# Regrouping exponent, score, attended-value and projection matmuls in a windowed attention kernel: bursts of three and three with six exponent buffers

## The chip, the cores and the metric

The kernel runs on one core of one Trainium2 chip, as one launch. The metric is the device time in microseconds. The core has five engines with queues of their own: TensorE (PE, with its weight loads shown as PEld), VectorE (DVE), ScalarE (ACT), GpSimd (POOL) and SyncE (SP), which here only issues DMAs. Each engine works through its own instructions in the order in which the program holds them, and waits on semaphores for the others.

## The reference

The input has 2048 tokens of 576 features. Four layers are added to it in turn: attention, spectral filter, attention, spectral filter.

```python
def _A_ref(x, wqkv, wo):
    B, S, D = x.shape
    H = 32; Dh = D // H; W = 256
    qkv = (x @ wqkv).reshape(B, S, 3, H, Dh).transpose(2, 0, 3, 1, 4)
    q, k, v = qkv[0], qkv[1], qkv[2]
    scores = jnp.einsum("bhqd,bhkd->bhqk", q, k) * (Dh ** -0.5)
    idx = jnp.arange(S)
    mask = (idx[:, None] - idx[None, :] >= 0) & (idx[:, None] - idx[None, :] < W)
    p = _softmax(jnp.where(mask[None, None], scores, -1e9), axis=-1)
    o = jnp.einsum("bhqk,bhkd->bhqd", p, v)
    return o.transpose(0, 2, 1, 3).reshape(B, S, D) @ wo

def _B_ref(x, w_r, w_i):
    X = jnp.fft.rfft2(x, axes=(-2, -1)) * (w_r + 1j * w_i)
    return jnp.fft.irfft2(X, s=x.shape[1:], axes=(-2, -1))

x = x + _A_ref(_layernorm(x), A_wqkv, A_wo)
x = x + _B_ref(_layernorm(x), B_w_r, B_w_i)
x = x + _A_ref(_layernorm(x), A_wqkv, A_wo)
x = x + _B_ref(_layernorm(x), B_w_r, B_w_i)
```

A query thus sees the 256 keys up to its own position, that is three tiles of 128 keys for each tile of 128 queries.

## The kernel before, in words

The program is written out by hand: every engine's order is the order of the calls in the Python code. `layer_a` is the attention, `layer_b` the spectral filter, and each is called twice. The change lies in `layer_a`, in its second part (from line 762 on), which the profile shows as the stretch of L801, L857, L889 and L909.

The 32 heads are taken in eight groups of four (`n`, `NQ` = 8), and a group in 16 tiles of 128 tokens (`i` or `j`, `NT` = 16). A step of the main loop (line 955) has a number t from -10 to 129, and x = t stands for the pair (group, tile) in order, 128 of them. A head has 18 features; a matrix of queries or keys stands in 64 rows, in which the high and the low part of the numbers lie one below the other. Two heads (`hp` = 0 and 1) stand in the upper and the lower 64 rows of the same tile, and `pair` tells two such couples apart. So four heads are two couples, and the matmuls of hp 0 and hp 1 use different halves of TensorE's rows.

These are the pieces of work of a step:

- `score_max(x, pair, hp)` (line 846): a matmul (L857, tile S, three PSUM buffers) gives the scores of 128 queries against up to 384 keys, and VectorE (L859) adds the mask and takes the row's maximum into `m`. It runs ten steps ahead (`LEAD` = 10).
- `m_rows(n, c)` (line 862): after four tiles a transpose (L865, tpm) turns the maxima into rows, ScalarE negates them (L867, mt) and four DMAs on SP (L872) put them into row 63 of each head's queries, so that the next matmul subtracts the maximum by itself. Line 864 takes the transpose's PSUM buffer from those of S.
- `exps(x, pair, hp)` (line 877): a matmul (L889, tile E, three PSUM buffers) gives the scores once more, keys in the rows and up to 384 queries in the columns, less the maximum; ScalarE (L890) takes the exponent into one of four places of tile P. After the fourth, two selections on POOL (L892 and L895) set what the mask excludes to zero. P has five buffers.
- `pv(x)` (line 900): sixteen short matmuls (L909) collect the attended values of four heads in U, one PSUM bank, in two halves: the keys of the tile before with 256 queries, and those of the tile itself or of the one before the last with 128. After four tiles ScalarE copies U out (L914, us). It runs two steps behind `exps`.
- `norm(n, c)` (line 916): four transposes (L919, tpo, in a buffer of S), a reciprocal (L922) and a product (L924) on VectorE, and a store on SP (L929).
- The steps of the projection (`pj`, line 943): 392 matmuls of 512 columns (L801), 14 to a block of queries or keys, into one PSUM bank. The 14th is followed by a cast on ScalarE (L813), and by `remainders()` (line 783), in which VectorE subtracts the cast (L816) and SP stores both parts (L818). The first 14 blocks' tile `sg` takes one of P's buffers. `goal` (lines 946 to 950) says how many projection matmuls are done by each step; 84 lie before t=2, and the other 308 are spread over t=2 to about t=102.
- `stack_load(n, c)` (line 824): twelve DMAs on SP (L833) that bring queries and keys of a group's quarter into place, twenty steps ahead. `v_load` brings the values. In the first layer 16 DMAs on POOL (line 992) copy constants to another place, one every four steps from t=32.

A step is written out by hand as: two exponents and two scores (hp 0 and 1 each), `pv(t-2)`, two exponents and two scores, about three projection steps, and then at most one of the `m_rows` and `norm` that are due:

```python
for pair in range(2):
    for hp in range(2):
        if 0 <= t < NX: exps(t, pair, hp)
    for hp in range(2):
        if t + LEAD < NX: score_max(t + LEAD, pair, hp)
    remainders()
    if pair == 0 and 0 <= t - 2 < NX: pv(t - 2)
for f in more: f()
```

A step whose t-2 begins a group (a multiple of 16) has no attended values, since the first tile's are taken with the second's.

Of the kernel before, what the change touches and what calls it, by code (L numbers as in the profile page):

```python
# [18 lines left out]
NT = 16  # L19
# [383 lines left out]
NQ = 8  # L403
# [205 lines left out]
def layer_a(tc, ident, eps, bp, src, dst, wqk_d, wv_d, wo_d, dc_d, gc_d, dram, copy, wvs, second, spectral, share):  # L609
# [17 lines left out]
    if True:  # L627
# [134 lines left out]
        with ExitStack() as c2:  # L762
# [24 lines left out]
            def proj(i, c, bank=0):  # L787

                box = {}
                ks = k_steps()  # L790
                cs = slice(c * 512, c * 512 + 512)

                def mm(s, k):
                    wk, p, xk = k
                    if s == 7 and c == 2 and 0 < i < 8:
                        w_split(i + 1)
                    if s == 0:
                        box["ps"] = pp.tile([128, 512], F32, tag="E" if bank else "pj", name=f"pj{i}_{c}", bufs=3 if bank else 1)
                    w = wt[i][0] if p == "h" else wt[i][1]
                    x = tokens(xT(xk, slice(0, S)), c) if second else xT(xk, cs)  # L800
                    T.matmul(box["ps"].rearrange("r (n p) -> r n p", n=NT) if second else box["ps"], w[:, wk], x, start=s == 0, stop=s == len(ks) - 1)  # L801
                    if s == len(ks) - 1:
                        if 4 * i + c < 14:

                            sg = wp.tile([128, 4, 384], F32, tag="P", name=f"sg{i}_{c}", bufs=5)
                            sg = sg.rearrange("r a b -> r (a b)")[:, 0:1024].rearrange("r (a t) -> r a t", a=2).bitcast(F32R)
                        else:
                            sg = wp.tile([128, 2, 512], F32R, tag="sg", name=f"sg{i}_{c}", bufs=2)
                        by, rest = box["ps"], sg
                        if second:  # L810
                            by = by.rearrange("r (n p) -> r p n", n=NT)
                            rest = sg.rearrange("r a (p n) -> r a p n", n=NT)
                        A.copy(rest[:, 0], by)  # L813

                        def remainder():
                            V.tensor_sub(rest[:, 1], by, rest[:, 0].bitcast(F32))  # L816
# [29 lines left out]
            def score_max(x, pair, hp):  # L846
# [30 lines left out]
            def exps(x, pair, hp):  # L877
# [19 lines left out]

            us = {}

            def pv(x):  # L900
                n, i = divmod(x, NT)

                e = i - i % 2
                for j in (i - 1, i - 2 + 2 * (i % 2)):
                    q0 = e if j < i else i
                    q1 = e + 2 if i - 1 == j else q0 + 1
                    for h in range(4):
                        if j >= 0:
                            T.matmul(U[32 * h:32 * h + 19, (q0 % 4) * 128:(q0 % 4) * 128 + 128 * (q1 - q0)], vts[n][:, j, h],  # L909
                                     pt[n, j][:, h, (q0 - j) * 128:(q1 - j) * 128],  # L910
                                     start=j == max(e - 1, 0), stop=j == i or (i == e and j == i - 2), skip_group_check=True)
                if i % 4 == 3:
                    us[n, i // 4] = u = wp.tile([128, 512], F32, tag="us", name=f"us{n}_{i}", bufs=1)
                    A.copy(u, U)  # L914

            def norm(n, c):
                tp = pp.tile([128, 4, 128], F32, tag="S", name=f"tpo{n}_{c}", bufs=3)
# [34 lines left out]
            OB = NX - 8  # L952
            out = Out(nc, ident, eps, bp, ov, o7v, srcv, dstv, wo_d, dc_d, gc_d)
# [1 line left out]
            for t in range(-LEAD, NX + 2):  # L955

                if t + LEAD in (0, 2):
                    stack_load(0, 2 + (t + LEAD) // 2)
                n, c = divmod(t + 20, NT)
                if c % 4 == 0 and 0 < n < NQ:  # L960
                    stack_load(n, c // 4)
                if t + LEAD == 5:
                    v_load(0)
                if t + 12 in range(NT, NX, NT):
                    v_load((t + 12) // NT)

                want = goal.get(t, len(pj))
                ends = done // 14 != want // 14
# [17 lines left out]
                    f()  # L986
                if t >= 1:
                    remainders()
                if copy and t >= 32 and t % 4 == 0 and t < 32 + 16 * len(copy):

                    z, r = divmod(t // 4 - 8, 4)
                    P.dma_start(*[a[32 * r:32 * r + 32] for a in copy[z]])

                y = t + LEAD - 1
                if 0 <= y < NX and y % 4 == 3:
# [102 lines left out]
```

## Time and profile before

| what | value |
|---|---|
| device time, median of three runs | 1575.02 us (1569.77 to 1582.44) |
| span of the profiled execution, first to last instruction | 1561.3 us |
| mean granted clock of TensorE | 0.993 |
| loop t=2 to t=103, first attention layer | 143.0 to 449.2 us |
| the same, second attention layer | 920.1 to 1226.6 us |

The profile is of one execution, whose span is 1561.3 us; its device time isn't listed by itself, and the median of the runs lies 13.7 us above that span. The rows of the profile name the line, the engine, the operation and the tiles as out<-in, then how many there were, their busy time and the mean of one; in the timeline a row begins with the start and the duration in microseconds, and rows of one kind that follow one another are merged. An entry in square brackets is idle time of that engine before the instruction, and what ended it. TensorE's matmuls overlap, and their ends are modelled, so distances between starts say more than durations. The stretches' rows give busy time of PE, PEld, DVE, ACT and POOL with the number of instructions in brackets.

### The profile page before, as it was taken

The numbers are of one execution on the slowest core, as the hardware profiler recorded it, in microseconds if no ns is written. First come the engines' busy times: TensorE is split into PE (matmuls) and PEld (weight loads), VectorE is DVE, ScalarE is ACT, GpSimd is POOL, SyncE is SP. The second block draws the span as 40 slices with busy tenths as digits, with TensorE's granted clock in tenths as the row PEclk, the third lists the DMA queues.
The fourth block names the chain that finished last, engine by engine and source line by source line (L and its number), as shares of the span: only waits on it lengthen the run. The fifth ranks groups of instructions, "written<-read, shape, count | busy, mean of one in ns | idle before, by whom it ended". The sixth has DMA issues, their size and how long they took to land.

```text
span 1561.3 us, 34502 instructions
## 1 busy us (share of the span) xinstructions
PE 1495.4 (96%) x12124; PEld 1086.4 (70%) x12124; DVE 976.1 (63%) x3152; ACT 806.4 (52%) x1900; POOL 624.6 (40%) x1026
## 2 busy tenths in 40 slices
PE   7999999999999899999999999999999998999998
PEld 7975555555555899858999755555555558998598
DVE  4327777777775555455852377777777755554577
ACT  5523666666667344323454246666666673442243
POOL 2172444444446233162321823443443563322434
PEclk9999999999999999999999999999999999999999
DMA  6656455555553456666764564555535543657664
GB/s 196 186 178 213 138 163 175 155 157 171 153 162 99 144 181 193 214 240 226 257 166 96 184 209 136 151 149 148 144 122 144 150 142 116 199 183 248 213 217 137
DMA packets 203130, 267.62 MB, mean 171 GB/s; under 512 B 103183, under 2 KB 108303, under 8 KB 201999
## 3 DMA queue, kind: packets, MB, share of 16 engines
q1 hardware_dynamic: 194638, 245.44, 51.8%
q10 hardware_dynamic: 7680, 15.59, 2.8%
q0 software_dynamic: 640, 4.39, 1.0%
q8 instruction: 97, 1.59, 0.4%
q14 instruction: 75, 0.61, 0.1%
HBM read 166.71 MB, written 102.00 MB: 172 GB/s over the span
## 4 chain that ended last, share of the span: by engine, by line
PE 70%; DVE 7%; DMA 6%; ACT 5%; POOL 5%; issue 1%; SPq 1%; POOLq 0%; DVEq 0%; ACTq 0%
PE pj L801 16%; PE U L909 11%; PE E L889 11%; PE S L857 7%; PE ops L555 6%; PE vps L738 4%; PE pf L202 3%; PE pz L215 3%; DMA ofree<-yd 2%; PE pi L361 2%; PE tpo L919 2%; ACT P L890 2%; PE po L382 2%; DVE ofree L298 1%; POOL uv L302 1%
## 5 line engine op out<-in xcount | busy, mean ns | idle before, releaser
L859 DVE CUSTOM_DVE_ANT_0 jk<-S,mask 128x384 bf16<-128x384 f32 (+2 forms) x1024 | 499.0, 529 | 148.8 <-PE S L857 146.0
L890 ACT ACTIVATE P<-E 128x384 f32<-128x384 f32 (+2 forms) x1024 | 423.2, 474 | 200.6 <-PE E L889 185.3
L892 POOL TENSOR_SCALAR_AFFINE_SELECT P<-P 128x512 f32<-128x512 f32 x256 | 163.0, 637 | 440.1 <-ACT P L890 438.0
L889 PE MATMUL E<-qs,ks 64*128 64x384 f32 (+2 forms) x1024 | 235.6, 429 | 12.4 <-ACT P L890 9.0
L857 PE MATMUL S<-ks,qs 63*128 63x384 f32 (+2 forms) x1024 | 212.3, 351 | 3.2 <-DVE m L859 2.4
L909 PE MATMUL U<-P,vq 128*19 128x128 f32 (+1 forms) x3840 | 204.9, 332 | 1.0 <-POOL P L895 1.0
L889 PEld LDWEIGHTS E<-qs,ks 64*128 64x128 f32 x1024 | 103.7, 184 | 145.3 <-ACT P L890 81.7
L909 PEld LDWEIGHTS U<-P,vq 128*19 128x19 f32 x3840 | 90.5, 98 | 101.3 <-issue 36.3
L801 PE MATMUL pj<-xh,wqh 128*128 128x512 f32 x360 | 158.0, 439 | 2.1 <-ACT vt L742 1.7
L895 POOL TENSOR_SCALAR_AFFINE_SELECT P<-P 128x512 f32<-128x512 f32 x224 | 142.6, 636 | 0.0
L857 PEld LDWEIGHTS S<-ks,qs 63*128 63x128 f32 x1024 | 116.5, 188 | 37.2 <-DVE m L859 27.1
L555 PE MATMUL ops<-oroom 128*128 128x288 f32 x840 | 120.8, 299 | 4.4 <-DVE oroom L538 3.0
L801 PE MATMUL pj<-xh,wql 128*128 128x512 f32 x360 | 122.9, 414 | 0.1
L801 PE MATMUL pj<-xl,wqh 128*128 128x512 f32 x288 | 120.9, 420 | 0.0
L555 PEld LDWEIGHTS ops<-oroom 128*128 128x128 f32 x840 | 112.8, 189 | 6.2 <-DVE oroom L538 4.0
L801 PEld LDWEIGHTS pj<-xh,wqh 128*128 128x128 f32 x360 | 68.0, 189 | 37.3 <-issue 24.2
L816 DVE TENSOR_TENSOR sg<-pj,sg 128x512 fp32r<-128x512 f32 x72 | 49.8, 691 | 61.8 <-ACT sg L813 61.8
L171 POOL TENSOR_TENSOR eo<-xn 128x287 f32<-128x287 f32 x32 | 26.1, 817 | 153.1 <-ACT xn L169 142.1
L859 DVE DVE_READ_ACCUMULATOR2_ANT m<- 128x1 f32 x1024 | 85.2, 83 | 0.0
L813 ACT CAST sg<-pj 128x512 fp32r<-128x512 f32 x72 | 42.4, 588 | 75.4 <-PE pj L801 73.8
L361 PE MATMUL pi<-oroom 128*128 128x256 f32 (+1 forms) x576 | 76.0, 285 | 5.4 <-ACT oroom L346 4.0
L801 PEld LDWEIGHTS pj<-xh,wql 128*128 128x128 f32 x360 | 64.7, 188 | 23.5 <-issue 13.5
(177 smaller groups left out, 2593.7 us busy)
## 6 DMA issues: line engine op xcount, KB each, us to landing
qk_d<-sg SPq DMA_DIRECT2D x56, 512.0 KB
qs<-qk_d SPq DMA_DIRECT2D x384, 72.0 KB
ks<-qk_d SPq DMA_DIRECT2D x384, 72.0 KB
v_d<-vt SPq DMA_DIRECT2D x32, 304.0 KB
vq<-v_d SPq DMA_DIRECT2D x16, 608.0 KB
yd<-ye SPq DMA_DIRECT2D x32, 290.0 KB
wt<-in_w SPq DMA_DIRECT2D x16, 580.0 KB
x<-ofree SPq DMA_DIRECT2D x32, 288.0 KB
```

Of the source, the lines that this page charges most:

```text
L361: T.matmul(o, z[:, sl, c, lo:lo + m], mo, start=k == 0, stop=k == 5)
L555: self.nc.tensor.matmul(self.ps[u][n][:, 0:288], x, self.w[p][:, wk * D + n * 288:wk * D + n * 288 + 288], start=first and i == 0, stop=la ...
L738: T.matmul(ps[:, n, 0:288], xT(xk, c), w[:, wk, n * 288:(n + 1) * 288], start=i == 0, stop=i == len(ks) - 1)
L801: T.matmul(box["ps"].rearrange("r (n p) -> r n p", n=NT) if second else box["ps"], w[:, wk], x, start=s == 0, stop=s == len(ks) - 1)
L816: V.tensor_sub(rest[:, 1], by, rest[:, 0].bitcast(F32))
L857: T.matmul(ps[:, 0:N], q[b:b + 63, pair, i * 128:i * 128 + 128], k[b:b + 63, pair, lo:hi], start=True, stop=True)
L859: V.tensor_tensor_reduce(out=jk[:, 0:N], in0=ps[:, 0:N], in1=mask[:, 384 - N:384], scale=1.0, scalar=-3e38, op0=ALU.add, op1=ALU.max, accu ...
L889: T.matmul(ps[:, 0:nq], k[b:b + 64, pair, j * 128:j * 128 + 128], q[b:b + 64, pair, j * 128:j * 128 + nq], start=True, stop=True)
L890: A.activation(p[:, hl_, 0:nq], ps[:, 0:nq], AF.Exp, scale=SC)
L892: P.affine_select(out=p[:, :, 0:128], in_=p[:, :, 0:128], pattern=[[0, 4], [1, 128]], compare_op=ALU.is_ge, fill=0.0, base=0, channel_mult ...
L895: P.affine_select(out=p[:, :, 256:384], in_=p[:, :, 256:384], pattern=[[0, 4], [-1, 128]], compare_op=ALU.is_gt, fill=0.0, base=0, channel ...
L909: T.matmul(U[32 * h:32 * h + 19, (q0 % 4) * 128:(q0 % 4) * 128 + 128 * (q1 - q0)], vts[n][:, j, h], pt[n, j][:, h, (q0 - j) * 128:(q1 - j) ...
```

## The change

The steps t=2 to t=103 (`MIX` = 104) leave the main loop and are written out by a new function, `bursts()`. The 408 exponents of these steps are taken in order, three at a time, and with each three go three scores, of the tile ten steps on and with the other half of the rows: a score, three exponents, two scores. So there are 136 bursts of six matmuls, in which the halves of the rows alternate. Between bursts stand the attended values and the projection steps in turn: after even bursts halves of `pv` (now `part(x, half)`), mostly three, and after odd bursts five, five or four projection steps, 14 in six bursts. At the starts of head groups an overflow rule puts some halves in front of projection steps. What is due of `norm` and `m_rows` follows the projection steps, up to two at a time, or all but the last where a block of 14 ends. The subtraction of the cast follows the scores of the next burst instead of standing before them. `loads(x)` and `copies(x)` stand ahead of the burst with tile x's first exponent. P has six buffers instead of five, and the room for it in SBUF comes from `dynamic_dma_scratch_size=8192`, a smaller room for the descriptors of POOL's DMAs than the one it has by default. The steps before t=2 and from t=104 on stay as they are, except that there too P has six buffers.

```diff
-                            sg = wp.tile([128, 4, 384], F32, tag="P", name=f"sg{i}_{c}", bufs=5)
+                            sg = wp.tile([128, 4, 384], F32, tag="P", name=f"sg{i}_{c}", bufs=6)
...
-                if t == hp == pair == 0:
+                if (n, c) not in ms:
...
-                    pt[n, j] = wp.tile([128, 4, 384], F32, tag="P", name=f"P{n}_{j}", bufs=5)
+                    pt[n, j] = wp.tile([128, 4, 384], F32, tag="P", name=f"P{n}_{j}", bufs=6)
...
-            def pv(x):
+            def part(x, half):
                 n, i = divmod(x, NT)
                 e = i - i % 2
-                for j in (i - 1, i - 2 + 2 * (i % 2)):
-                    q0 = e if j < i else i
...
+                j = (i - 1, i - 2 + 2 * (i % 2))[half]
+                q0 = e if j < i else i
...
-                if i % 4 == 3:
+                if half and i % 4 == 3:
                     us[n, i // 4] = u = wp.tile([128, 512], F32, tag="us", name=f"us{n}_{i}", bufs=1)
                     A.copy(u, U)
+
+            def pv(x):
+                part(x, 0)
+                part(x, 1)
...
-            for m in range(22):
-                a, b = [2 + 23 * z // 5 for z in (m, m + 1)]
-                for t in range(a, b):
-                    goal[t] = 84 + 14 * m - (-14 * (t + 1 - a) // (b - a))
+            MIX = 104
...
+            def bursts():
+                es = [(x, pair, hp) for x in range(2, MIX) for pair in range(2) for hp in range(2)]
+                ss = [(x + LEAD, pair, 1 - hp) for x, pair, hp in es]
+                left = [*(5, 5, 4) * 20, *(4, 4, 3, 3) * 2]
+                gaps = {}
+                for p in range(2 * MIX - 5):
+                    g = 2 * ((p + 1) // 3)
+                    if p % 8 == 0 and p and (p + 1) % 3:
+                        g += (p + 1) % 3
+                    elif p % 8 == 1 and p > 1 and (p + 1) % 3 == 2:
+                        g += 1
+                    gaps.setdefault(g, []).append(divmod(p, 2))
+                at = done
+                for k in range(len(es) // 3):
+                    e, c = es[3 * k:3 * k + 3], ss[3 * k:3 * k + 3]
+                    for x, pair, hp in e:
+                        if pair == hp == 0:
+                            loads(x)
+                            copies(x)
+                    score_max(*c[0])
+                    for f in e:
+                        exps(*f)
+                    score_max(*c[2])
+                    score_max(*c[1])
+                    remainders()
+                    for x, half in gaps.get(k, ()):
+                        part(x, half)
+                        if half and x % 4 == 3:
+                            due.append((norm, *divmod(x // 4, 4)))
+                    full = (3 * k + 3) // 4 + 11
+                    if (3 * k) // 4 + 11 < full and full % 4 == 3:
+                        due.append((m_rows, *divmod(full // 4, 4)))
+                    if k % 2:
+                        m = left.pop(0)
+                        for f in pj[at:at + m]:
+                            f()
+                        ends, at = at // 14 != (at + m) // 14, at + m
+                        for f, *a in due[:len(due) - 1 if ends else 2]:
+                            f(*a)
+                            due.pop(0)
+                remainders()
+                part(MIX - 3, 1)
+                return at
...
             for t in range(-LEAD, NX + 2):
...
+                if 2 <= t < MIX:
+                    if t == 2:
+                        due.append((m_rows, 0, 2))
+                        done = bursts()
+                    continue
+                loads(t)
...
-    nc = bacc.Bacc("TRN2", target_bir_lowering=False, num_devices=1)
+    nc = bacc.Bacc("TRN2", target_bir_lowering=False, num_devices=1, dynamic_dma_scratch_size=8192)
```

More of the change, by code (lines that the diff above doesn't have):

```diff
@@ L946, in layer_a, with loads @@
             goal = {t: -(-70 * (t + LEAD + 1) // 9) if t < -1 else (75, 80, 84)[t + 1] for t in range(-LEAD, 2)}
-            for m in range(22):
-                a, b = [2 + 23 * z // 5 for z in (m, m + 1)]
-                for t in range(a, b):
-                    goal[t] = 84 + 14 * m - (-14 * (t + 1 - a) // (b - a))
[L952 to L958, printed above, removed]
+            MIX = 104
+            def loads(t):
                 n, c = divmod(t + 20, NT)
@@ L965, in layer_a, with copies @@
                     v_load((t + 12) // NT)
+            def copies(t):
+                if copy and t >= 32 and t % 4 == 0 and t < 32 + 16 * len(copy):
+                    z, r = divmod(t // 4 - 8, 4)
+                    P.dma_start(*[a[32 * r:32 * r + 32] for a in copy[z]])
+            def bursts():
[41 more added lines that the diff above has]
+                return at
@@ L967, in layer_a @@
+            OB = NX - 8
+            out = Out(nc, ident, eps, bp, ov, o7v, srcv, dstv, wo_d, dc_d, gc_d)
+            for t in range(-LEAD, NX + 2):
+                if t + LEAD in (0, 2):
+                    stack_load(0, 2 + (t + LEAD) // 2)
+                if 2 <= t < MIX:
[4 more added lines that the diff above has]
+                loads(t)
                 want = goal.get(t, len(pj))
```

15 lines of the change are left out of this document (6 added, 9 removed).

## The prediction

> **What bounds the kernel now.** I read the page's head first, then the busy times of the stretches of the run, then TensorE's own timeline inside one step of the loop that the change rewrites.
>
> ```profile
> span 1561.3 us, 34502 instructions
> PE 1495.4 (96%) x12124; PEld 1086.4 (70%) x12124; DVE 976.1 (63%) x3152; ACT 806.4 (52%) x1900; POOL 624.6 (40%) x1026
> 143.00:449.20 306.20, 302.93 (x2766) 169.06 (x2766) 227.75 (x884) 200.88 (x485) 132.53 (x212) 0.99 0.53 159
> 920.10:1226.60 306.50, 302.99 (x2768) 168.41 (x2768) 227.32 (x885) 201.09 (x485) 124.31 (x195) 0.99 0.51 145
> ```
>
> The last two rows are the steps t=2 to t=103 of the first and the second attention layer; they give length, then busy time of PE, PEld, DVE, ACT and POOL, then granted clock, DMA share and GB/s. TensorE is taken up for 303 of 306 us, the next engine, VectorE, for 228. So 612.7 us of the span are the changed loop, TensorE sets its length, and VectorE (228) and ScalarE (201) are floors far below. A step is 306.2/102 = 3.00 us. One step of TensorE:
>
> ```profile
> 387.39 0.28 PE L865 MATMUL tpm<-ident,m 128*16 128x128 f32 x1
> 387.60 0.44 PE L889 MATMUL E<-qs,ks 64*128 64x384 f32 x2
> 387.88 0.33 PE L857 MATMUL S<-ks,qs 63*128 63x384 f32 x2
> 388.14 0.85 PE L909 MATMUL U<-P,vq 128*19 128x256 f32 x16
> 388.92 0.44 PE L889 MATMUL E<-qs,ks 64*128 64x384 f32 x2
> 389.20 0.34 PE L857 MATMUL S<-ks,qs 63*128 63x384 f32 x2
> 389.47 0.50 PE L801 MATMUL pj<-xh,wql 128*128 128x512 f32 x1
> 389.80 0.40 PE L801 MATMUL pj<-xh,wqh 128*128 128x512 f32 x1
> 390.04 0.39 PE L801 MATMUL pj<-xh,wql 128*128 128x512 f32 x1
> 390.36 0.44 PE L889 MATMUL E<-qs,ks 64*128 64x384 f32 x2
> ```
>
> Starts alone are read here, since ends overlap. Two exponent (E) and two score (S) matmuls, one of each pair per half of the array's rows, take 0.54 to 0.55 us until the next kind starts (387.60 to 388.14, 388.92 to 389.47). Attended values (U) take 0.78 (388.14 to 388.92), three projection steps (pj) 0.89 (389.47 to 390.36), though the last two pj start only 0.24 apart. Each block thus carries a surplus at its edge, and the changed order has fewer blocks. The surplus of an E/S block needs its pitch without an edge. One place shows it: where a step has no attended values, two fours run together.
>
> ```profile
> 384.71 0.44 PE L889 MATMUL E<-qs,ks 64*128 64x384 f32 x2
> 384.99 0.34 PE L857 MATMUL S<-ks,qs 63*128 63x384 f32 x2
> 385.17 0.34 PE L889 MATMUL E<-qs,ks 64*128 64x384 f32 x1
> 385.73 0.44 PE L889 MATMUL E<-qs,ks 64*128 64x384 f32 x1 [0.22 <-ACT P L890]
> 386.36 0.50 PE L801 MATMUL pj<-xl,wqh 128*128 128x512 f32 x1
> ```
>
> The second pair starts 0.28 after the first, the third only 0.18 after the second (385.17), and then the fourth exponent waits for one of three buffers (385.73). So pairs cost 0.18 each inside a block, and a block 0.55 - 2 x 0.18 = 0.19 on top.
>
> **The change, term by term, per layer.**
>
> E/S blocks: 102 steps had two each, less seven places (x-2 a multiple of 16) where both run together: 197. Now 136 bursts of six. 61 x 0.19 = 11.6 us gained. A burst of six should take 0.55 + 0.18 = 0.73.
>
> pj blocks: one per step (102) become one per two bursts (68). For the surplus, compare a block of two steps:
>
> ```profile
> 404.40 0.50 PE L801 MATMUL pj<-xh,wqh 128*128 128x512 f32 x1
> 405.06 0.44 PE L889 MATMUL E<-qs,ks 64*128 64x384 f32 x2
> ```
>
> Two steps take 0.66 and three 0.89: 0.23 a step and 0.20 a block. 34 x 0.20 = 6.8 us gained.
>
> U blocks: 95 (102 less the seven) become 74: 67 even gaps, six odd ones that the overflow rule fills, and the last half. The surplus of a U block is not visible in a row; it lies between 388.14 - 387.88 - 0.18 = 0.08, what the E/S row loses after its last pair, and 0.20, that of pj. I take 0.13, near the middle because its neighbours on both sides are E/S blocks: 21 x 0.13 = 2.7 us (1.7 to 4.2). Blocks in sum: 21.1 us.
>
> The changed loop keeps its transposes, and what ScalarE and VectorE do beside them:
>
> ```profile
> 401.19 0.97 PE L801 MATMUL pj<-xh,wql 128*128 128x512 f32 x3
> 401.99 0.60 PE L919 MATMUL tpo<-ident,us 128*128 128x128 f32 x4
> 402.52 0.45 PE L889 MATMUL E<-qs,ks 64*128 64x384 f32 x2
> L914 ACT COPY us<-U 128x512 f32<-128x512 f32 x25 | 14.7, 587 | 1.2
> L813 ACT CAST sg<-pj 128x512 fp32r<-128x512 f32 x22 | 13.0, 590 | 2.4 <-PE pj L801 2.3
> L816 DVE TENSOR_TENSOR sg<-pj,sg 128x512 fp32r<-128x512 f32 x23 | 15.9, 692 | 9.0 <-ACT sg L813 9.0
> 389.39 0.88 ACT L890 ACTIVATE P<-E 128x384 f32<-128x384 f32 x2 [0.39 <-PE E L889]
> 385.18 1.64 ACT L890 ACTIVATE P<-E 128x384 f32<-128x384 f32 x4 [0.41 <-PE E L889]
> 389.57 0.56 DVE L859 CUSTOM_DVE_ANT_0 jk<-S,mask 128x384 bf16<-128x384 f32 x1 [0.29 <-PE S L857]
> 390.06 0.55 DVE L859 CUSTOM_DVE_ANT_0 jk<-S,mask 128x384 bf16<-128x384 f32 x1
> L924 DVE TENSOR_TENSOR o<-tpo,rc 128x288 f32<-128x288 f32 x24 | 11.0, 457 | 0.8
> ```
>
> The first three rows give the transposes (0.53 at 401.99, less 0.10 because the pj block before them is 0.80 instead of 0.89; the maxima likewise 0.21 - 0.09 at 387.39). They stay as they are, in the sum before as after.
>
> Waits that go: the nominal loop is 95 x 2 x 0.55 + 7 x 0.91 + 95 x 0.78 + 102 x (0.20 + 3.02 x 0.23) for E/S, merged E/S, U and pj (308 steps), plus 24 transposes of results at 0.43 and 26 of maxima at 0.11 = 289.4. The loop took 306.2, so 16.8 us are waits, the merged places first (384.71 to 386.36 is 1.65 for a nominal 0.91).
>
> Waits that come. (a) A burst uses all three E buffers. ScalarE starts 0.47 after an exponent's matmul (388.92 to 389.39), takes 0.44 each (0.88/2), and TensorE goes on 0.12 after a release (385.18 + 0.43 to 385.73). So the third exponent of the next burst, 0.28 into it, can start 0.47 + 3 x 0.44 + 0.12 = 1.91 after this burst began: a burst every 1.63 us or more. After a full gap of U (three halves, about 1.1) the next burst comes after 1.83, after pj (0.20 + 4.67 x 0.23 = 1.28) after 2.01: no wait. Eight gaps per layer hold one U half alone (0.35): bursts 1.08 apart, 0.55 lost each, 4.4 us; those at the head groups' starts cost some 1.8 more. (b) VectorE subtracts the projection's cast (0.69) after the next burst's three maxima, which start 0.37 after a score (389.20 to 389.57) and follow one another by 0.49 (389.57 to 390.06): done at about 0.37 + 1.47 + 0.69 = 2.53 after that burst's start, and the next pj group, which has one bank, starts at 0.73 + 1.1 + 0.73 = 2.56. No slack: 0.1 at 16 ends, 0.45 at the six where a norm sits on VectorE too (its product alone is 0.46): 4.3 us. (c) The maxima's rows reach qs by DMA. In two places per layer they now come 1.5 steps ahead of the exponents that read them, and behind 12 loads on SP (after bursts 61 and 109: m_rows(3,1), m_rows(5,2)).
>
> ```profile
> 380.00 2.49 SPq L833 DMA_DIRECT2D qs<-qk_d  x6
> 382.54 2.69 SPq L833 DMA_DIRECT2D ks<-qk_d  x6
> 910.78 0.26 ACT L867 ACTIVATE mt<-tpm 16x128 fp32r<-16x128 f32 x1
> 916.45 2.51 SPq L872 DMA_DIRECT2D qs<-mt  x4
> 920.12 0.18 PEld L889 LDWEIGHTS E<-qs,ks 64*128 64x128 f32 x1 [2.59 <-issue]
> ```
>
> Twelve loads take SP 5.2 us to issue. The last three rows show the same collision in the second layer's start today: the maxima were ready at 911.04, SP came to them at 916.45, the exponent started 3.67 later, after 2.59 of standstill. At burst 61, with times from burst 60: SP starts the loads at some 3.0 (behind the projection's store, which waits for (b)), the rows at 8.2, the exponent at 11.9, where TensorE arrives at 8.45: 3.5 us lost; at burst 109, with one more load, some 4.5. Behind the late rows on SP stand only those of the next four steps and a result's store, which nobody waits for so soon. With 0.8 for two near misses: 8.8 us.
>
> ```profile
> L892 POOL TENSOR_SCALAR_AFFINE_SELECT P<-P 128x512 f32<-128x512 f32 x101 | 64.2, 636 | 172.9 <-ACT P L890 172.8
> L992 POOL DMA_DIRECT2D dcr<-in_dc x4 | 2.3, 579 | 0.0
> dcr<-in_dc POOLq DMA_DIRECT2D x4, 362.5 KB, 5.0
> ```
>
> At nothing: the sixth P buffer and the later U halves. POOL's two masks of 0.64 end two bursts before their readers, and POOL is idle over half of the loop; if that cover is gone, each U block waits up to 1.3. The smaller scratch for POOL's own DMAs: its 16 copies lie in the first layer only, and now stand up to a step earlier among the masks. No row prices a smaller scratch: the bounds are nothing and a full landing of 5.0 for each, 80 us on POOL, which its idle time of 306.2 - 132.5 = 174 covers at both ends; I take nothing, being the nearer to today's 0.58 us an issue. The order within SP moves by a burst or so; besides (c) no exponent comes near its rows. The 24 steps after t=103 and all outside the loop are the same instructions.
>
> Sum per layer: 21.1 + 16.8 - (4.4 + 1.8 + 4.3 + 8.8) = 18.6 us; two layers 37. The span would go from 1561.3 to 1524. The profile tells no time of its execution beside the span; the median of the runs, 1575.02, lies 13.7 above it, and I take that as constant: 1538 us.
>
> **Rivals.** First, the waits that come are hidden, all but the thin gaps: 2 x (21.1 + 16.8 - 6.2) = 63 gained, 1512 us. For it: 16.8 us of waits today come from two bursts with one spare buffer; against it: the arithmetic of (c), which has its precedent at 920.12.
>
> Second, the pitch of 0.18 isn't kept in a mixed burst and every pair costs 0.28, as the second pair does today. Then each burst is 0.10 longer, 136 x 0.10 = 13.6 us a layer, and the gain shrinks to 2 x 5.0: 1565 us. For it stands the 0.28 at 384.99, against it 385.17, one stream only. The Trainium skill (TensorE: Matmul & The Clock Gate, Part 3) says a weight load overlaps running matmuls only where its row group differs, and third-pair loads share theirs with the pair ahead. By that rule the time would be this rival's; the 0.18 here speaks against it, the 0.28 for it.
>
> Third, on the other side: the three E buffers become the bound. The place is the third exponent of each burst; it decides when the mean distance between bursts passes 306.2/136 = 2.25 us, where I expect 2.11. With 2.40, that is when ScalarE's other pieces (0.59 for us or sg) fall into most bursts' chains of 1.63, the loop is 326 us and the kernel 1615. Against it: us and sg together are 47 pieces for 136 bursts, and ScalarE has a third of the loop free. The Trainium skill (TensorEngine Tiling (Array Packing), Performance Considerations) warns that packing speeds the matmuls and not the emptying of PSUM; the floors of 228 and 201 us say that it doesn't bind here on average.
>
> Fourth, late maxima spread: eight such collisions a layer instead of two, 24 us more each: 1586 us. Against it: elsewhere the rows come 2 to 6 steps ahead.
>
> **How the numbers follow.** The forecast with some of its waits more or less (1520 to 1557) has 0.57, the first rival 0.13, the second 0.12, the third 0.10, the fourth 0.08. A measurement tells 1% from no change, that is 1559 and 1591. Faster: 0.57 + 0.13 + 0.05 of the second = 0.75; same: 0.07 + 0.07 of the fourth = 0.14; slower 0.11. The range leaves out the third and fourth: 1510 to 1572.
>
> **What would show it.** Loop windows of 280 to 294 us each; six E/S starts spanning 0.73 to the next kind, pairs 0.28 and then 0.18 apart; 1.9 to 2.1 between bursts with full gaps; exponents at x=50 and x=86 of each layer standing 3 us or more for qs<-mt; the wait of exponents for ScalarE no longer than before. Wrong would be: pairs 0.28 apart throughout, bursts over 2.25 apart, or a loss outside the loop.

## The result, and the profile after

| kernel | median of 20 runs each | lowest to highest | span of the profiled execution | its granted clock |
|---|---|---|---|---|
| before | 1569.87 us | 1564.79 to 1587.50 | 1561.3 us | 0.993 |
| after | 1581.31 us | 1574.33 to 1587.43 | 1574.2 us | 0.978 |

The ratio is 1.006 [1.004, 1.008]: no faster, where 1538 us and a range of 1510 to 1572 had been forecast. The forecast was wrong. One profile below, that of e3, is of an execution well above that kernel's median (1570.95 us against 1559.41), and e3's ratio leaves it out. In the kernel after, the lines of `norm` are L923, L926 and L928, four further on than before. The head of the page of the kernel after, and then the busy times in its two loops (length, then busy time of PE, PEld, DVE, ACT and POOL, granted clock, DMA share, GB/s):

```profile
span 1574.2 us, 34565 instructions
PE 1486.6 (94%) x12124; PEld 1122.2 (71%) x12124; DVE 967.2 (61%) x3152; ACT 795.4 (51%) x1900; POOL 622.9 (40%) x1026
```

```profile
144.30:451.20 306.90, 293.62 (x2771) 183.77 (x2771) 222.50 (x887) 195.46 (x486) 131.73 (x212) 0.97 0.53 159
924.40:1234.70 310.30, 295.77 (x2769) 183.64 (x2769) 222.33 (x885) 195.30 (x486) 124.03 (x196) 0.97 0.50 143
```

From the loop's first exponent to the first behind it pass 306.9 and 310.3 us, as against 306.2 and 306.5 before and some 288 in the forecast. TensorE is busy for 9.3 and 7.2 us less, although more of its work ran at half clock. But before it stood for 3.3 and 3.5 us of a loop, and now for 13.3 and 14.5, and its clock went from 0.99 to 0.97. TensorE's timeline in the kernel after, at a place where nothing disturbs it (start, duration, engine, line, tiles):

```profile
153.56 0.44 PE L857 MATMUL S<-ks,qs 63*128 63x384 f32 x1
153.56 0.62 PE L889 MATMUL E<-qs,ks 64*128 64x384 f32 x3
154.02 0.34 PE L857 MATMUL S<-ks,qs 63*128 63x384 f32 x2
154.29 1.06 PE L909 MATMUL U<-P,vq 128*19 128x128 f32 x24
155.28 0.44 PE L857 MATMUL S<-ks,qs 63*128 63x384 f32 x1
```

The six exponents and scores take 0.73 (153.56 to 154.29), as forecast, and the next burst begins 1.72 after this one. Compare with a burst that follows `norm`, again in the kernel after, first on TensorE, then on VectorE:

```profile
169.45 0.60 PE L923 MATMUL tpo<-ident,us 128*128 128x128 f32 x4
169.98 0.44 PE L857 MATMUL S<-ks,qs 63*128 63x384 f32 x1
169.98 0.62 PE L889 MATMUL E<-qs,ks 64*128 64x384 f32 x3
170.44 0.33 PE L857 MATMUL S<-ks,qs 63*128 63x384 f32 x1
170.98 0.41 PE L857 MATMUL S<-ks,qs 63*128 63x384 f32 x1 [0.21 <-DVE o L928]
171.32 1.05 PE L909 MATMUL U<-P,vq 128*19 128x256 f32 x19
```

```profile
170.08 0.26 DVE L926 RECIPROCAL rc<-tpo 128x16 f32<-128x16 f32 x1 [0.58 <-PE tpo L923]
170.37 0.46 DVE L928 TENSOR_TENSOR o<-tpo,rc 128x288 f32<-128x288 f32 x1
```

The last two scores start together 0.46 after the burst's start in the undisturbed one. Here one starts at 170.44 and the last at 170.98, 0.54 later. The transposes `tpo` hold one of the three S buffers until VectorE's product ends (170.37 + 0.46 = 170.83), and a burst has three scores: the third needs that buffer. The bracket shows only 0.21 of it, because it counts from the end of the score before (170.44 + 0.33 = 170.77). So starts tell the price, and the groups by wait understate it. There are 25 such places in a loop. By their starts, the 25 bursts of the first loop take 1.12 to 1.35, in sum 13.6 us more than 25 x 0.73.

The late maxima, in the kernel after: TensorE, then SP's queue, then the page's busy times and the clock around the second such place.

```profile
283.65 0.43 PE L857 MATMUL S<-ks,qs 63*128 63x384 f32 x1
286.74 1.13 PE L889 MATMUL E<-qs,ks 64*128 64x384 f32 x3 [2.65 <-DMA qs<-mt]
...
392.13 0.32 PE L857 MATMUL S<-ks,qs 63*128 63x128 f32 x1
398.34 1.13 PE L889 MATMUL E<-qs,ks 64*128 64x384 f32 x3 [5.89 <-DMA qs<-mt]
```

```profile
277.81 2.45 SPq L833 DMA_DIRECT2D qs<-qk_d  x6
280.30 3.17 SPq L833 DMA_DIRECT2D ks<-qk_d  x6
283.74 3.73 SPq L872 DMA_DIRECT2D qs<-mt  x6
```

```profile
395.00:405.20 10.20, 6.86 (x43) 4.13 (x45) 1.59 (x10) 3.40 (x8) 1.69 (x3) 0.50 0.45 145
```

SP issues the rows right behind twelve loads and TensorE stands for 3.09 us (283.65 to 286.74) and 6.21 (392.13 to 398.34): forecast in place, less so in size. Nobody had forecast the last fence: behind the standstill the granted clock is 0.50 for 10.2 us, of which 6.9 lie in work (the 10.2 us begin within the standstill).

### The profile page after: what moved, and what is told of

It is laid out like the page before. It is cut to its first block, busy times and chain, and to the rows that moved or that the text cites. A ratio compares the mean times of both kernels' runs of the same rounds, so it can differ in the third digit from the quotient of the medians.

```text
span 1574.2 us, 34565 instructions
## 1 busy us (share of the span) xinstructions
PE 1486.6 (94%) x12124; PEld 1122.2 (71%) x12124; DVE 967.2 (61%) x3152; ACT 795.4 (51%) x1900; POOL 622.9 (40%) x1026
## 4 chain that ended last, share of the span: by engine, by line
PE 70%; DVE 8%; DMA 7%; ACT 4%; POOL 2%; issue 2%; SPq 1%; POOLq 0%; DVEq 0%; ACTq 0%
PE pj L801 15%; PE S L857 11%; PE U L909 10%; PE ops L555 6%; PE E L889 5%; PE vps L738 4%; PE pf L202 3%; PE pz L215 3%; PE tpo L923 2%; PE pi L361 2%; PE pq L313 2%; PE po L382 2%; PE p L294 2%; DMA ofree<-yd 1%; DMA qs<-mt 1%
## 5 line engine op out<-in xcount | busy, mean ns | idle before, releaser
L859 DVE CUSTOM_DVE_ANT_0 jk<-S,mask 128x384 bf16<-128x384 f32 (+2 forms) x1024 | 492.4, 528 | 159.5 <-PE E L889 83.7
L890 ACT ACTIVATE P<-E 128x384 f32<-128x384 f32 (+2 forms) x1024 | 411.3, 477 | 194.3 <-PE E L889 167.1
L857 PE MATMUL S<-ks,qs 63*128 63x384 f32 (+2 forms) x1024 | 294.1, 385 | 8.0 <-DVE o L928 6.6
L889 PE MATMUL E<-qs,ks 64*128 64x384 f32 (+2 forms) x1024 | 233.1, 387 | 28.3 <-DMA qs<-mt 20.7
L857 PEld LDWEIGHTS S<-ks,qs 63*128 63x128 f32 x1024 | 151.6, 190 | 123.6 <-DVE m L859 66.0
L909 PE MATMUL U<-P,vq 128*19 128x128 f32 (+1 forms) x3840 | 200.0, 335 | 1.1 <-POOL P L895 0.5
L889 PEld LDWEIGHTS E<-qs,ks 64*128 64x128 f32 x1024 | 116.6, 190 | 59.3 <-issue 31.3
L801 PE MATMUL pj<-xh,wqh 128*128 128x512 f32 x360 | 151.8, 422 | 4.3 <-ACT vt L742 1.7
L909 PEld LDWEIGHTS U<-P,vq 128*19 128x19 f32 x3840 | 93.9, 99 | 80.1 <-issue 33.6
L801 PEld LDWEIGHTS pj<-xh,wql 128*128 128x128 f32 x360 | 64.3, 191 | 25.2 <-issue 13.7
```

Source lines behind the costliest of these rows:

```text
L857: T.matmul(ps[:, 0:N], q[b:b + 63, pair, i * 128:i * 128 + 128], k[b:b + 63, pair, lo:hi], start=True, stop=True)
L859: V.tensor_tensor_reduce(out=jk[:, 0:N], in0=ps[:, 0:N], in1=mask[:, 384 - N:384], scale=1.0, scalar=-3e38, op0=ALU.add, op1=ALU.max, accu ...
L889: T.matmul(ps[:, 0:nq], k[b:b + 64, pair, j * 128:j * 128 + 128], q[b:b + 64, pair, j * 128:j * 128 + nq], start=True, stop=True)
L890: A.activation(p[:, hl_, 0:nq], ps[:, 0:nq], AF.Exp, scale=SC)
```

## The experiments

Four theories came out of the traces. N: the transposes of `norm` hold the third S buffer. R: the maxima's rows stand on SP behind twelve loads. C: each standstill is followed by a stretch of half clock, so it costs more than its own length. Their rival P: the burst order itself, or the P buffer and the smaller scratch, costs the time. All experiments compute the whole result.

**e1: norm inside the gap.** Edit to the kernel after (core):

```diff
-                        for f in pj[at:at + m]:
+                        ends = at // 14 != (at + m) // 14
+                        now = due[:len(due) - 1 if ends else 2]
+                        del due[:len(now)]
+                        for f in pj[at:at + 2]:
                             f()
-                        ends, at = at // 14 != (at + m) // 14, at + m
-                        for f, *a in due[:len(due) - 1 if ends else 2]:
-                            f(*a)
-                            due.pop(0)
+                        for f, *a in now:
+                            if f is norm:
+                                f(*a)
+                        for f in pj[at + 2:at + m]:
+                            f()
+                        at += m
+                        for f, *a in now:
+                            if f is m_rows:
+                                f(*a)
```

> The changed kernel, with the transposes of norm moved from behind the projection steps of a gap to behind the second of them, so that VectorE frees their S buffer before the next burst. Theory A (the last score of a burst waits for the buffer that norm's transposes hold): in the 25 bursts per layer that follow a norm the last score starts 0.46 us into the burst instead of 0.9 to 1.0, each loop is 12 to 14 us shorter, and the kernel takes some 1555 us against 1581. Rival (VectorE as a whole is late, and the buffer only shows it): the last score still starts at 0.8 or later, another wait for VectorE takes its place, and no more than 4 us go.

Measured: 1561.74 us, 0.9969 [0.9942, 0.9995] of the kernel before. The loops take 297.3 and 298.2 us, 9.6 and 12.1 less than after; that is less than expected in the first loop, and the whole is some 7 us slower than expected. The page's group of scores in the kernel after, and then in e1 (busy, mean ns | idle before, releaser):

```profile
L857 PE MATMUL S<-ks,qs 63*128 63x384 f32 (+2 forms) x1024 | 294.1, 385 | 8.0 <-DVE o L928 6.6
```

```profile
L857 PE MATMUL S<-ks,qs 63*128 63x384 f32 (+2 forms) x1024 | 279.9, 385 | 0.2
```

N holds: the wait for the product `o` is gone. The late rows of R stay (the two bursts take 3.40 and 6.39 us more than 0.73 in the first layer).

**e2: loads two tiles later.** Edit to the kernel after:

```diff
-                            loads(x)
+                            if x >= 4:
+                                loads(x - 2)
```

> The changed kernel, with the twelve loads of queries and keys issued two tiles later, so that no rows of maxima stand behind them on SP. Theory B (the rows of maxima come late at x=50 and x=86, and TensorE's standstill there also brings the half clock that the trace shows right behind): the two waits of 3.1 and 6.2 us per layer shrink to under 1 us, the granted clock in both loops goes from 0.97 back to 0.99, each loop is 11 to 15 us shorter, the kernel some 1555 us. Rival (the bursts themselves bring the lower clock): the waits shrink, but the clock stays at 0.97 and the loops gain 9 us or less, 1563 us or more.

Measured: 1568.39 us, 1.002 [0.9996, 1.0044]; loops of 308.6 and 301.7. The standstills at x=50 and x=86 are gone. Others of 3.0 to 3.8 us took their place, so that the 11 to 15 us a loop that were expected did not come. Here is one on TensorE in e2:

```profile
165.95 0.61 PE L889 MATMUL E<-qs,ks 64*128 64x384 f32 x2
170.35 0.41 PE L889 MATMUL E<-qs,ks 64*128 64x384 f32 x1 [3.79 <-DMA qs<-mt]
```

So R's mechanism is right (moving the loads moves the standstill), but the cure is not: SP's order has rows near loads elsewhere too.

**e3: e1 and e2 together.**

> Both edits together. Theories A and B: the gains add, since one is a wait for a PSUM buffer and the other for a DMA in other bursts: both loops at 278 to 284 us, the kernel some 1530 us, 2.5% under the kernel before. Rival (one common slack, VectorE or the DMA queue, sets the pace): the sum stays well under the two alone, 1548 us or more.

Measured: 1559.41 us, 0.9946 [0.9912, 0.9979]. In the profiled execution of 1570.95 us the loops fall to 295.9 and 293.8, but the stretch behind each, up to the last exponent, is 68.6 and 72.4 us long, in the kernel after 57.1 and 60.1. ScalarE and then TensorE show where:

```profile
1233.77 0.67 ACT L506 CAST oroom<-ofree 128x576 fp32r<-128x576 f32 x1 [5.25 <-DMA ofree<-in_wo]
```

```profile
1229.59 0.44 PE L889 MATMUL E<-qs,ks 64*128 64x384 f32 x1
1234.88 0.69 PE L889 MATMUL E<-qs,ks 64*128 64x384 f32 x1 [4.86 <-ACT P L890]
```

A cast of the output weights (line 506), put in ScalarE's queue at t=108, waits for a load that SP issues behind the twelve loads. The exponents queue behind the cast. This is a further wait, which e9 tests.

**e4: the P buffer and the scratch alone.** Edit to the kernel before: `bufs=6` for both tiles of P, and `dynamic_dma_scratch_size=8192`.

> The kernel before, with six P buffers and the smaller scratch for POOL's DMAs alone. Theory: neither costs nor gains anything, within 3 us of the kernel before. Rival (the scratch or the place of the buffers in SBUF costs what was not found in the loop, part of the 11 us that the changed kernel lost): 5 us slower or more, most of it in the first layer where POOL issues its copies.

Measured: 1567.76 us, 1.001 [0.9983, 1.0037]. The loops take 304.8 and 306.7 us, as before. So the sixth buffer and the scratch cost 0.4% at most, and this part of P falls.

**e5: norm inside, rows first.** Edit to e1: what is due is sorted before it is taken, so that the maxima's rows do not queue behind a norm.

```diff
+                        due.sort(key=lambda d: d[0] is norm)
```

> The first experiment's kernel, with the maxima's rows taken ahead of norm among what is due, so that they come 3 to 3.5 steps ahead at x=10, 50, 82 and 86 and ahead of the twelve loads. Theories A and B with the clock: the standstills at x=50 and x=86 go, with the half clock behind them, the loops take 282 to 286 us instead of 297, and the kernel comes 1.5 to 2.2% under the kernel before. Rival (the lower clock belongs to the bursts as such): the loops lose the 10 us of standstill alone, the mean clock stays at 0.975 or below, and the kernel is at most 1.2% under.

Measured: 1537.16 us, 0.9794 [0.9753, 0.9835]. A norm between projection steps, the burst behind it, and the loops, in e5:

```profile
173.06 0.60 PE L923 MATMUL tpo<-ident,us 128*128 128x128 f32 x4
173.41 0.48 PE L801 MATMUL pj<-xh,wqh 128*128 128x512 f32 x1
...
174.28 0.44 PE L857 MATMUL S<-ks,qs 63*128 63x384 f32 x1
174.28 0.62 PE L889 MATMUL E<-qs,ks 64*128 64x384 f32 x3
174.74 0.34 PE L857 MATMUL S<-ks,qs 63*128 63x384 f32 x2
```

```profile
143.10:427.90 284.80, 283.75 (x2769) 177.23 (x2769) 223.88 (x887) 193.40 (x486) 132.09 (x212) 0.99 0.56 170
898.20:1184.10 285.90, 283.89 (x2769) 176.44 (x2769) 224.09 (x887) 193.35 (x486) 124.50 (x196) 0.99 0.53 156
```

Both scores start at 0.46 again (174.74), TensorE stands for 1 to 2 us of a loop, and the clock is back at 0.99. With the same bursts in the same order as in the kernel after, the loops are 22 and 24 us shorter: P falls altogether.

**e6: and the last loads later.** Edit to e5, meant to free the rows behind the loop:

```diff
-                            loads(x)
+                            if x != 100:
+                                loads(x - 3 if x == 103 else x)
```

> The kernel with norm inside and rows first, and the loads of the eighth group's third quarter three tiles later, behind the rows of (6,3), which in the second layer came late behind them (up to 4.9 us of standstill at x=110, then half clock in the steps after the loop). Theory: the steps after t=103 take 55 to 57 us in both layers, and the kernel is 3 to 10 us faster than the one without this edit. Rival (the half clock of those steps is chance, whatever comes ahead of it): no difference beyond 3 us.

Measured: 1551.65 us, 0.9884 [0.9835, 0.9932]: worse than e5, against what was expected. The loops keep their 285.3 and 285.9, but the stretches behind them grow to 69.6 and 69.9 us. The chain in e6: SP comes to the output weights late, ScalarE's cast stands for them, TensorE's exponent stands for ScalarE.

```profile
442.14 2.10 SPq L833 DMA_DIRECT2D qs<-qk_d  x6
...
446.53 0.84 SPq L502 DMA_DIRECT2D ofree<-in_wo  x2
```

```profile
453.47 0.67 ACT L506 CAST oroom<-ofree 128x576 fp32r<-128x576 f32 x1 [10.63 <-DMA ofree<-in_wo]
454.04 0.86 ACT L890 ACTIVATE P<-E 128x384 f32<-128x384 f32 x2
...
454.58 0.69 PE L889 MATMUL E<-qs,ks 64*128 64x384 f32 x1 [10.23 <-ACT P L890]
```

From 445.9 on the clock is 0.50 for 20.5 us. The reason given for e6 (rows late behind the loop) was wrong: it is this cast.

**e7: rows first alone.** The line of e5, in the kernel after, without e1's edit.

> The changed kernel with the rows first and norm left where it is. Theory B: the standstills of 3.1 and 6.2 us at x=50 and x=86 and the half clock behind them go, some 13 us per layer, mean clock up by 0.005 or more, the kernel some 0.8% under the kernel before (about 1.6% less than the changed one). Rival (as in the experiment with later loads, the queue finds another victim): standstills over 2 us at other tiles, no more than 0.3% under the kernel before.

Measured: 1563.22 us, 0.9955 [0.9928, 0.9983], where 0.992 was expected; loops of 298.6 and 300.1. The late rows are gone, the wait for `o` is not (12.0 us by the page, 6.6 after). So from after, R's cure alone takes 8.3 and 10.2 us off the loops, N's alone (e1) 9.6 and 12.1, both 22.0 and 24.4. From e7 to e5, where only N's cure differs, the loops fall by 13.7 and 14.2: N's price per layer. From e1 to e5, where only R's cure differs, they fall by 12.4 and 12.3: R's price, with the half clock behind it.

**e8: standstills put into the kernel before.** Its rows of two quarters are written a second time, shortly before their readers (the writing is moved out of `m_rows` into a function `rows`, which moves the lines behind it on by seven: L889 becomes L896):

```diff
...
+                if t in (50, 86):
+                    g = {50: (3, 1), 86: (5, 2)}[t]
+                    rows(*g, mts[g])
```

> The kernel before, with the rows of maxima of two quarters written a second time, the same numbers, right ahead of x=50 and x=86 in each layer, so that TensorE stands still there for about 4 us, four times in all. Theory (a standstill is followed by half clock, which costs once more): 2 x 2 standstills of some 4 us plus half clock of 6.8 us behind each, which costs half of that, 26 us or more in sum, mean clock 0.01 lower. Rival (the standstill costs itself alone): 16 us or less, clock unchanged.

Measured: 1601.09 us, 1.0218 [1.0182, 1.0254], 31 us more. The standstills are longer than meant, since the second writing too came behind twelve loads. One of them on TensorE in e8, and the clock behind it:

```profile
289.00 0.40 PE L801 MATMUL pj<-xh,wqh 128*128 128x512 f32 x1
294.45 1.01 PE L896 MATMUL E<-qs,ks 64*128 64x384 f32 x2 [5.06 <-DMA qs<-mt]
```

```profile
293.30:300.10 6.80, 5.65 (x21) 3.50 (x25) 2.00 (x8) 2.25 (x6) 1.22 (x2) 0.50 0.01 1
```

The four standstills last 5.13, 8.55, 4.09 and 7.50 us, 25.3 in sum, and behind each lie 6.8 or 10.2 us of half clock. The loops grew by 17.6 and 19.1, that is 36.7: 11.4 more than the standstills, some 3 us behind each. In these four stretches TensorE works 25.9 us at half clock, of which half, 12.9, is lost: near the 11.4. C holds in a kernel that knows neither bursts nor six buffers.

**e9: the casts two steps later.** Edit to e5:

```diff
-                if 0 <= t - (OB - 12) < 10 and (t - (OB - 12)) % 2 == 0:
-                    out.split((t - (OB - 12)) // 2)
+                if 0 <= t - (OB - 10) < 10 and (t - (OB - 10)) % 2 == 0:
+                    out.split((t - (OB - 10)) // 2)
```

> The norm inside the gap, the maxima's rows first, and besides the five casts of the output weights (ScalarE, line 506) two steps later, at t=110 to 118 instead of 108 to 116. Theory: behind the loop ScalarE stands in its queue for the output weights' load (2.3 us at worst with rows first and norm inside), the exponents queue behind that cast, and TensorE stands 1.93 us at 1200.9 of that run, after which 10.2 us are granted half the clock. Then the waits of the cast for the load go, the standstill goes, the rest of the second layer behind the loop falls from 61.9 to 57 us, and the median from 0.979 to about 0.976 of the kernel before. Rival: the maxima's rows set that place; then TensorE stands as long at the same exponent, for the rows, and the time stays.

Measured: 1518.36 us, **0.9699 [0.9666, 0.9732]**, the fastest of all and more than expected. The stretch behind each loop is 55.1 us, the cast's wait is gone, and TensorE has its full clock all through the second loop but for its start, and far beyond it (clock in the row's third number from the end), over a span of 1513.8 us:

```profile
898.00:1360.00 462.00, 449.93 (x4234) 317.93 (x4233) 325.38 (x1188) 284.69 (x702) 200.28 (x350) 1.00 0.53 157
```

**e10: e6 with the casts at t=115 to 119.**

> The last loads later, as in the run that stood 10.2 and 8.8 us behind its loops, with the five casts of the output weights at t=115 to 119. Theory: those standstills were the cast's wait for a load that SP issued late, with the exponents queued behind it on ScalarE. Then both go but for what the rows of maxima, issued behind the same loads, hold up at x=112: 2 to 4 us each. The rest behind the loop falls from 69.6 and 69.9 to some 61 us, the median from 0.988 to about 0.978. Rival: the rows alone made them; then the standstills stay at 8 to 10 us, named for the rows.

Measured: 1535.40 us, 0.9806 [0.9765, 0.9847], as against e6's 0.9884. The stretches behind the loops fall to 61.1 and 67.9 us. The standstills of 10.2 and 8.8 us shrink to 3.87 and 4.29, and these are named for the rows, as the theory had it:

```profile
453.43 1.01 PE L889 MATMUL E<-qs,ks 64*128 64x384 f32 x2 [3.87 <-DMA qs<-mt]
...
1213.08 1.06 PE L889 MATMUL E<-qs,ks 64*128 64x384 f32 x2 [4.29 <-DMA qs<-mt]
```

## Why the prediction was wrong

**Blocks: right.** The pitch of 0.18 is kept and a burst takes 0.73 (first burst shown above), so the second rival falls. Adding up all blocks of a loop at their lengths under full clock gives some 270 us a layer, about 20 less than the same count gives for the kernel before; 21.1 were forecast.

**Old waits that go: right but for a part; the third rival falls.** In the first loop of the kernel before, the exponents' weight loads waited for ScalarE 101 times and 32.7 us; in the kernel after it is this, with the other waits of the loop that matter here (total, times, longest):

```profile
PEld pj L801 <- DVE sg L816: 4.6, 14, 0.4
...
PEld E L889 <- ACT P L890: 2.0, 10, 0.2
```

Of the 16.8 us of waits, though, 3.4 in the first layer and 1.7 in the second were half clock at the loop's start, and the kernel after has 1.7 and 3.3 there: this part didn't go. The mean distance between bursts is 2.26 and 2.28 us (306.9/136, 310.3/136), just over the 2.25 that the prediction named as a sign of the third rival; but it is not the E buffers that set it, as the last row shows.

**Wait (a): right in size, the cause in part another; wait (b): too large.** The subtraction's waits are 4.6 us by the rows of the first loop for a forecast 4.3, but by starts the 13 bursts ahead of such a projection step that don't follow a single half of U lose only 1.7 us in sum. In the second loop the rows give one wait of 0.4 us for a weight load and six, 1.3 us in sum, for matmuls. A burst behind a thin gap, in e5, first on TensorE, then one of its weight loads:

```profile
178.49 0.44 PE L857 MATMUL S<-ks,qs 63*128 63x384 f32 x1
...
179.62 0.44 PE L857 MATMUL S<-ks,qs 63*128 63x384 f32 x1
179.62 0.74 PE L889 MATMUL E<-qs,ks 64*128 64x256 f32 x3
180.06 0.91 PE L857 MATMUL S<-ks,qs 63*128 63x384 f32 x2
180.90 0.85 PE L909 MATMUL U<-P,vq 128*19 128x256 f32 x16
```

```profile
180.53 0.18 PEld L857 LDWEIGHTS S<-ks,qs 63*128 63x128 f32 x1 [0.29 <-DVE m L859]
```

It starts 1.13 after its predecessor and takes 1.28 instead of 0.73: 0.55 lost, the forecast's number, but here by luck. The forecast let the third exponent wait for ScalarE and the E buffers; in this burst the last score waits for VectorE's maximum and an S buffer (180.53). Of the ten bursts behind a single half of U in this loop, two are of this kind; in six the third exponent starts 0.70 to 0.95 into the burst, waiting for ScalarE as forecast, and two are in between. Together the ten lose 5.8 us, for a forecast of 6.2 with the head groups. **At nothing**, P's sixth buffer and the scratch: right (e4).

**Late rows (c): right place, size too small.** The exponents at x=50 and x=86 start 3.09 and 6.21 us behind their burst's first score in the first layer and 2.94 and 6.47 in the second, 9.3 and 9.4 a layer for a forecast 8.0 (8.8 with two near misses). So the first rival, in which these waits are hidden, falls, and so does the fourth with its eight places a layer. And the half clock behind them wasn't in the price at all. After 286.74 some 5.9 us of work run at half clock, after 398.34 some 6.9, and half of each is lost: 2.9 + 3.4 = 6.3 a layer.

The Trainium skill (TensorE: Matmul & The Clock Gate, Why this matters for your kernels) advises against idle gaps of TensorE above some 3 us between bursts, because the clock then falls to half; Part 1 of the same page of the Trainium skill gives the gate's window as 3.4 us. The trace agrees: stretches of 6.8 and 10.2 us, whole multiples of 3.4, at 0.50, behind standstills of 3.09 and 6.21. It doesn't confirm 3 us as a sharp bound: in e5 a standstill of 1.93 us at 1200.91 is followed by 10.2 us of half clock:

```profile
1201.70:1211.90 10.20, 9.74 (x68) 4.99 (x72) 6.54 (x25) 4.56 (x15) 4.17 (x6) 0.50 0.03 5
```

The prediction had four collisions of 3.5 and 4.5 us in its sum and charged their length only.

**The step that failed** is the one on the transposes: "They stay as they are, in the sum before as after." Their own time does. But the transposes of results take an S buffer, and a burst now asks for all three at once, where a block of the old order asked for two. The prediction counted the three E buffers in this way, but not the three S buffers. No wait (d) for this stood among the waits that come. It costs 13.6 us a layer by the starts of the first loop, 13.7 and 14.2 by e7 to e5. With the 6.3 of half clock, which stood at nothing too, that is 19.9, more than the 18.6 us a layer that the forecast gained.

The sum for the first layer, then: 270 for blocks, 9.3 for late rows, 6.3 for the half clock behind them, 13.6 for norms, 5.0 for thin gaps, 1.7 for the subtraction, and 1.7 for half clock at the loop's start, that is about 308, measured 306.9. It is an account from rows, good to a few us: the cures of R and N together took 22.0 us off this loop, less than the 29.2 of the three terms that they cure. Of the difference, 1.7 us are a longer half clock at the start of e5's loop, and another part is a wait of N's kind that the cure of R brings. The transpose of the maxima takes an S buffer too, and with the rows first it often lies just behind the end of a projection block, whose cast ScalarE does before it reads the transpose (in e5 the transpose at 270.15, the cast at 270.35, the reading at 270.83). So the last score behind it waits, in e5's first loop (total, times, longest):

```profile
PEld S L857 <- ACT mt L867: 1.6, 5, 0.3
```

By starts these five bursts take 1.16 instead of 0.73, 2.1 us in sum. The rest of the difference isn't accounted for.

**Outside the loop** the forecast had nothing, and in the profiled executions 8 us came (1574.2 - 617.2 = 957.0, before 948.6). Part of it is the cast's wait for the output weights, 2.6 us in two places after and 1.1 before. How much of the rest is half clock behind it and how much varies from run to run, one execution doesn't tell; e4, with the loop of before, has 956.3 outside its loops.

**The base** was off too. The 13.7 us between the first three runs' median and the profiled span aren't constant: in all executions with both numbers the time is 1.7 to 2.1 us above the span. The rest goes, as far as the record shows, with the clock: the profiled execution of before ran at 0.993, and 35 later runs of that kernel have a mean of 0.990. The clocks of the first three runs aren't on record.

**What the forecast's order was worth** shows in e9, where the norm wait, the late rows and the cast's wait are cured and, of the waits named here, (a), (b) and that for the transposed maxima stay. Without (c) the forecast's sum is 2 x (21.1 + 16.8 - 6.2 - 4.3) = 55 us off 1561.3, that is 1506; e9's span, at a clock of 0.995, is 1513.8. Its loops take 283.5 and 286.1 us, where that sum gives 279 each.

## What to carry to other kernels

When work is grouped into larger bursts, count for each ring of buffers what the burst takes at once, and then everything else that draws from the same ring, such as transposes: here the burst's last member waited for the engine that empties them. On an in-order DMA queue, and on an engine that casts what a DMA brings, look at what stands ahead of the piece on the critical path, because a faster loop brings readers closer to transfers that haven't moved. Price a standstill of TensorE by its length and the half clock behind it, and look for one just behind the changed loop too.

## What the runs showed of the hardware that was not expected

- Half clock is a large part of the differences. 35 runs of the kernel before went from 1556.01 us at a mean clock of 0.995 to 1576.47 at 0.983; 20 runs after had a mean of 0.974. Within one kernel 0.01 of clock goes with 9 to 14 us.
- A small wait can start a long slow stretch. From e5 to e9 one group of casts moves by two steps, the standstill of 1.93 us goes, and the median falls by 1.0% of the time before, in separate comparisons (0.9794 to 0.9699). Not all of it is that standstill's: the profiled spans differ by 13.0 us, of which 8.9 lie in the stretches behind the loops. The mean clock of the runs went from 0.980 to 0.993. Why stretches of half clock lasted as long as 27.3 us in e10 and 23.9 in e6 stays open; short waits for ScalarE (0.2 to 0.5 us each) recur there, but they recur in e9 too, at full clock.
- Four transposes cost 0.35 us between two projection steps (173.06 to 173.41) and 0.53 ahead of a burst (169.45 to 169.98).
